# Fewer filler products at the start, and the left-over rows of the last four batches in output order

## The chip, the cores and the metric

The kernel runs on one core of one Trainium2 chip. Its engines work side by side, each on its own stream of instructions: TensorE (PE) for matrix products, VectorE (DVE) and ScalarE (ACT) for element-wise work, GpSimd (POOL) and SyncE (SP), which here mostly issue transfers. ACT also has a queue from which it issues transfers. The metric is the device time of one execution in microseconds (us). The kernel before takes 240.45 us, the median of 3 runs from 239.67 to 241.16.

## The reference

```python
B, H, S, D = q.shape                  # 8, 8, 576, 64
m = 32
scale = 1.0 / np.sqrt(D)
q_lm = q.reshape(B, H, m, S // m, D).mean(axis=3)
k_lm = k.reshape(B, H, m, S // m, D).mean(axis=3)
A  = softmax(scale * q    @ k_lm.T)
Bm = softmax(scale * q_lm @ k_lm.T)
C  = softmax(scale * q_lm @ k.T)
Z = Bm.T / (norm1(Bm) * norminf(Bm) + 1e-06)
for _ in range(6):
    Z = 2 * Z - Z @ Bm @ Z
attn = A @ Z @ C @ v
x = attn.transpose(0, 2, 1, 3).reshape(B * S, H * D)    # 4608 x 512
h = x @ w_in                                            # 512 x 2048
g = h * (1.0 / (1.0 + np.exp(-h)))
out = g @ w_out                                         # 2048 x 512, float32
```

This is an attention with 32 landmarks per head, whose small inverse is found by six iterations, followed by a two-layer network with a silu between the layers.

## The kernel before

Every step is an operation with a name (`A(name, engines, emit, deps, ...)`), and a text, `SEQUENCE`, lists the names in the order in which each engine gets its instructions; nothing reorders them afterwards. A word `*n` in it puts n filler products on PE: a product of a tile of zeros (`zer`, 128x128) with 256 columns of zeros into a PSUM bank that is not otherwise used at that time. A word such as `c21@5740.0/DVE` picks the engine where there is a choice.

Per batch (the number behind the dot), `attn` builds transposed queries and keys, landmark sums (`lms`, `lmc`, `ltr`, `lmT`), the small softmax (`sb`, `pb`), the exponentials of A (`A`, `Ax`) and of C (`C`, `Cx`), the normalisation of A (`S` on PE, `Ln` and `Rs` on ACT, `etn` on DVE), and the iterations (`ns` on PE, `nsd` and `fb` on DVE). From `cv`, `wc`, `zbd`, `zt` comes a small matrix per head, and `m0` to `m3` multiply it with the first layer's weights, so that the first layer is one product of `etn` with `m`. `layer1` runs that product, in operations `h0` to `h15` for 512 of the 576 rows of a batch; `g0` to `g15` are the silu of each on ACT, written to `gm`.

A batch has 576 = 32 x 18 rows: row 18 l + j belongs to landmark l and place j. The 512 rows are j from 0 to 15. The 64 left-over rows, j = 16 and 17, go through `hx0` and `hx8`, and the silu `gx0` and `gx8` writes them to `gx`, where four batches stand side by side: 64 columns each, first the 32 rows of j = 16, then those of j = 17. After batches 3 and 7 the second layer takes `gx` as a group of 256 rows.

The second layer (`layer2_pair`) takes 256 rows as an upper and a lower half of 128 and halves of the weights, and forms the output with seven products (`p1` to `p7`) instead of eight, with sums of operands on DVE (`ss0` to `ss3`). The copies and additions c1, u2, c11, c12, c5, c22, c21 bring the products from PSUM into two output tiles of 128 x 512: c11 completes the left 256 columns of the first tile, c12 its right columns, c22 the right columns of the second tile, c21 its left columns. Transfers (`store`) then write rows to memory. Each takes 32 rows with the same j, since consecutive l lie 18 output rows apart. For the last batch's tiles, four transfers per tile alternate between the queues of SP and ACT (`spread`), and for the very last pair, that of `gx` (named 5740 and 5741), the first tile goes as eight transfers of 32 rows x 256 columns and the second as four of 32 x 512.

Transfers of SP and ACT share eight completion counters: each transfer gets one, and is issued only when the earlier transfer with that counter has landed.

The fillers before stand at these places: 15 at the very start, 6 and 6 during the first transposes, 1 ahead of `ltr0.0`, 6 ahead of `sb.0`, 5 ahead of `C.0`, 2 ahead of `ltr1.1`, and from there to `h4.0` 22 in ten places among the iterations of batch 0 and the exponentials of batch 1, and 1 more ahead of `h13.0`; 64 in all.

Of the kernel before, what the change touches and what calls it, by code (L numbers as in the profile page):

```python
# [10 lines left out]
AF = mybir.ActivationFunctionType  # L11
# [13 lines left out]
lmT0.0/ACT *6 sb.0 pb.0 trc014.0/DVE trc09.0/DVE A.0 Ax01.0 Ax00.0 Ax10.0 Ax11.0 *5 C.0 Cx01.0  # L25
# [6 lines left out]
tr10.1 trc10.1/ACT tr15.1 *2 ltr1.1 lmT1.1/ACT fb20.0 nsd21.0 etn1.0 trc15.1/DVE ns20.0 fb31.0 *3  # L32
ns31.0 ctm10.0 trc114.1/ACT etn0.0 nsd31.0 sb.1 pb.1 *1 A.1 Ax01.1 Ax00.1 nsd20.0 fb30.0 pbs.1
wrc.0 *1 ns30.0 nsd30.0 ctc10.0/DVE fb40.0 pbr.1 fb41.0 bmx.1 bmt.1 wi3b1 Ax11.1 Ax10.1 *5 C.1
Cx00.1 Cx11.1 Cx01.1 *1 ns40.0 nsd40.0 ns41.0 nsd41.0 fb50.0 fb51.0 cv0.0 cv1.0 wc.0 S01.1 Ln01.1
ns50.0 nsd50.0 *2 ns51.0 bbd.1 nsd51.0 zbd.0 S11.1 Ln11.1 S00.1 Ln00.1 wi2b0 wi2b1 wi2a ldv0.1
ldv1.1 *5 zt.0 ztc.0/DVE S10.1 ctm00.1 ctc00.1/DVE Rs0.1 Ln10.1 Cx10.1 *2 m1.0 mc11.0/ACT
mc10.0/DVE m0.0 f0.1 mc01.0/DVE mc00.0/ACT *1 ctm10.1 ctc10.1/DVE Rs1.1 csb.1 *1 h4.0 n1.1 m3.0
nrm.1 stz.1 stf0.1 mc31.0/DVE fb00.1 g4.0 mc30.0/DVE h2.0 g2.0 h6.0 g6.0 h0.0 g0.0 h3.0 ns00.1
wrc.1 nsd00.1 fb10.1 h5.0 g5.0 m2.0 mc21.0/ACT mc20.0/DVE *1 h13.0 g13.0 ns10.1 nsd10.1 fb20.1  # L40
h15.0 hx0.0 g15.0 ns20.1 nsd20.1 fb30.1 h9.0 g9.0 h11.0 g11.0 etn0.1 ns30.1 nsd30.1 fb40.1 hx8.0
gx8.0 g3.0 h8.0 h12.0 g12.0 etn1.1 ns40.1 nsd40.1 fb50.1 gx0.0 h10.0 g10.0 ld1.2 tr15.2
trc15.2/DVE h14.0 g14.0 ns50.1 nsd50.1 zbd.1 ldv2.1 cv0.1 wc.1 tr114.2 trc114.2/DVE tr19.2
trc19.2/DVE zt.1 g8.0 ztc.1/ACT tr10.2 trc10.2/DVE lra1.2 h7.0 g7.0 m3.1 mc31.1/ACT mc30.1/ACT
m1.1 mc11.1/DVE mc10.1/ACT h1.0 g1.0 ld0.2 tr00.2 lrb1.2 tr09.2 tr014.2 trc014.2/DVE tr05.2
trc05.2/DVE trc09.2/DVE lrc1.2 trc00.2/ACT h12.1 g12.1 h7.1 g7.1 h15.1 m2.1 mc20.1/ACT m0.1
mc00.1/ACT mc21.1/ACT mc01.1/ACT wo0 o0@5001.0 h14.1 g14.1 g15.1 o0@5000.0 fold lrd1.2 lra0.2
lrb0.2 lrc0.2 lrd0.2 h11.1 g11.1 ltr0.2 ltr1.2 lmT1.2/DVE lmT0.2/ACT ss00@5020.0 ss10@5020.0
ss20@5020.0 ss30@5020.0 wo1 h5.1 o1@5000.0 sb.2 pb.2 pbs.2 pbr.2 bmx.2 bmt.2 wo2 wt00 bbd.2 h8.1
h3.1 o1@5001.0 o2@5000.0 wo3 o2@5001.0 wt01 g8.1 csb.2 o3@5001.0 oc@5001.0/ACT g3.1 g5.1 n1.2  # L50
nrm.2 stz.2 o3@5000.0 hx8.1 f0.2 gx8.1 h0.1 g0.1 oc@5000.0/ACT h2.1 h10.1 g10.1 h4.1 h1.1 g2.1
g1.1 wt11 wt21 stf0.2 fb00.2 ns00.2 h13.1 g13.1 wt31 nsd00.2 fb10.2 wt10 wt20 wt30 p1@5020.0
c1@5020.0/ACT ns10.2 nsd10.2 fb20.2 h9.1 h6.1 g4.1 g9.1 g6.1 ss00@5100.0 p5@5020.0 c5@5020.0/DVE
hx0.1 gx0.1 ss10@5100.0 l1done.0 C.2 Cx00.2 Cx10.2 p6@5020.0 u2@5020.0/DVE ld100.3 ld101.3 ld110.3
ld111.3 ldv1.3 xt10.3<ldv1.3 xt11.3<ldv1.3 ns20.2 nsd20.2 ss20@5100.0 p3@5020.0 c12@5020.0
p7@5020.0 ld000.3 ld001.3 ld010.3 ld011.3 xt01.3<ldv1.3 xt00.3<ldv1.3 ldv0.2 ldv2.2 ldv1.2
l1done.1 A.2 Ax01.2 Cx11.2 ct1.2<ldv1.3 Ax10.2 Ax11.2 p1@5100.0 c1@5100.0/ACT Ax00.2 Cx01.2
ct0.2<ldv1.3 os@5000.0 ld100.4<ct0.2 ld101.4 ld110.4 ld111.4 lra1.3 fb30.2 ns30.2 p2@5020.0
ss30@5100.0 lrb1.3 os@5001.0 S10.2 S11.2 Ln11.2 Ln10.2 Rs1.2 p6@5100.0 S01.2 Ln01.2 S00.2 Ln00.2
p5@5100.0 nsd30.2 lrc1.3 fb40.2 lrd1.3 ltr1.3 c22@5020.0 lra0.3 u2@5100.0/DVE lrb0.3 p4@5020.0  # L60
ns40.2 lrc0.3 lrd0.3 ltr0.3 c11@5020.0 etn1.2 nsd40.2 c5@5100.0/ACT p3@5100.0 Rs0.2 lmT1.3/ACT
etn0.2 lmT0.3/ACT sb.3 c12@5100.0 c21@5020.0/ACT p7@5100.0 pb.3 pbs.3 pbr.3 fb50.2 A.3 Ax11.3
cv0.2 ldv1.4<xt00.3 c22@5100.0 wrc.2 wc.2 ld000.4<xt00.3 ld001.4 ld010.4 ld011.4 ldv0.3 ldv2.3
ldv2.4<xt00.3 ns50.2 nsd50.2 Ax10.3 Ax00.3 S11.3 Ln11.3 Ax01.3 p2@5100.0 C.3 Cx00.3 Cx01.3 Cx10.3
zbd.2 zt.2 ztc.2/ACT S10.3 Ln10.3 p4@5100.0 Cx11.3 ss00@5120.0 c11@5100.0 os@5100.0 ss10@5120.0
ss20@5120.0 p1@5120.0 S01.3 Ln01.3 m3.2 mc31.2/ACT bmx.3 wrc.3 mc30.2/DVE c21@5100.0/ACT os@5101.0
ct1.3<ldv1.4 m2.2 mc21.2/DVE mc20.2/ACT bmt.3 p5@5120.0 S00.3 m0.2 m1.2 mc11.2/DVE csb.3 bbd.3
n1.3 nrm.3 stz.3 c1@5120.0/ACT p6@5120.0 u2@5120.0/DVE mc01.2/ACT mc10.2/ACT Rs1.3 Ln00.3 Rs0.3
mc00.2/ACT h14.2 f0.3 h12.2 p2@5120.0 stf0.3 fb00.3 ns00.3 nsd00.3 c5@5120.0/DVE fb10.3 c11@5120.0
g12.2 p7@5120.0 h7.2 g7.2 ns10.3 nsd10.3 h4.2 h5.2 h8.2 g8.2 g5.2 fb20.3 ns20.3 h10.2 g10.2  # L70
c22@5120.0 p4@5120.0 c21@5120.0/ACT nsd20.3 fb30.3 ns30.3 hx0.2 nsd30.3 fb40.3 h15.2 gx0.2 g15.2
ns40.3 nsd40.3 ct0.3<ldv1.4 xt00.4<ldv1.4 h9.2 g9.2 g14.2 h1.2 h0.2 g1.2 g0.2 fb50.3 ss30@5120.0
ns50.3 nsd50.3 zbd.3 h11.2 g11.2 h13.2 h3.2 cv0.3 h2.2 wc.3 g4.2 g13.2 g3.2 etn1.3 zt.3 ztc.3/DVE
etn0.3 p3@5120.0 c12@5120.0 m3.3 mc30.3/ACT m0.3 mc01.3/DVE mc00.3/ACT m2.3 mc21.3/ACT m1.3
mc20.3/ACT hx8.2 g2.2 h6.2 g6.2 mc31.3/DVE h12.3 gx8.2 h3.3 h10.3 mc10.3/DVE mc11.3/DVE h7.3 h2.3
g2.3 h4.3 g4.3 g10.3 h13.3 h5.3 g5.3 hx8.3 gx8.3 g13.3 h9.3 h11.3 g7.3 h14.3 h6.3 g6.3 g11.3
p1@5200.0 g3.3 h8.3 g8.3 ss00@5200.0 p5@5200.0 hx0.3 g14.3 g9.3 ss00@5220.0 xt11.4<ldv1.4
xt01.4<ldv1.4 xt10.4<ldv1.4 ld100.5<xt10.4 ld101.5 ld110.5 ld111.5 ldv0.4 ldv1.5 ld000.5 ld001.5
# [175 lines left out]
def kernel(  # L254
# [43 lines left out]
    def bank(o, i=0):  # L298
        return banks[o.slot[i]]
# [54 lines left out]
    A = P.add  # L354
# [546 lines left out]
    def layer1(b):  # L901
# [5 lines left out]
        for dc in range(NDC):  # L907
# [20 lines left out]
            if dc % 8 == 7:  # L928
                d0 = dc - 7
                cell = {}  # L930

                def xm(e, d0=d0, cell=cell):
                    ps = bank(cell["o"]).rearrange("p (c x) -> p c x", c=8)
                    for d in range(8):
                        for g in range(NG):
                            mm(ps[:, d].rearrange("p (c x) -> p c x", c=2),
                               m_sb[:, g, (d0 + d) * 128:(d0 + d + 1) * 128],
                               etc[:, g, :, 256:288], start=(g == 0), stop=(g == 1))
                o = cell["o"] = A(f"hx{d0}.{b}", [("PE", mm_us(64, 16))], xm,
                                  etn_ops[b] + m_ops[b, d0 // 4] + m_ops[b, dc // 4]  # L940
                                  + l2_last.get(("x", b // 4 - 1), []), p + 0.5, psum=1, cls="L1")
                pes.append(o)
                c = (b % 4) * 64
                gx_ops[b].append(A(
                    f"gx{d0}.{b}", [("ACT", act_us(512))],
                    lambda e, d0=d0, cell=cell, c=c: nc.scalar.activation(  # L946
                        out=gx[:, d0:d0 + 8, c:c + 64],
                        in_=bank(cell["o"]).rearrange("p (c x) -> p c x", c=8), func=AF.Silu),
                    [o], p + 0.5, table="silu").reads(o))
# [36 lines left out]
    def store(e, t, place, m, cols=slice(0, DMODEL)):  # L986
# [101 lines left out]
    def layer2_batch(b):  # L1088
# [10 lines left out]
        if b % 4 == 3:  # L1099
# [3 lines left out]
                [[(x, j) for x in (y, y + 1) for j in (J - 2, J - 1)] for y in (b - 3, b - 1)],  # L1103
# [69 lines left out]
```

## Time and profile before

| | |
|---|---|
| median of the runs | 240.45 us |
| the profiled execution's own time | 239.41 us |
| its span, first to last instruction | 237.4 us |
| PE busy | 231.4 us, 2948 products |
| DVE busy | 183.0 us |
| ACT busy | 182.1 us |
| the 64 fillers | 1.1 to 31.0 us |
| written to memory | 9.44 MB |

A span is divided in the profile's page into 40 slices with the busy share of each engine, and the chain of work that ended last is followed back from the last instruction. PE counts as busy while it waits with a product begun, so its share is to be read together with the waits of the engines that use its results. Times in the timeline are from the span's start. In a timeline row stand start, duration, engine, line, operation, output and inputs, shape and count, and behind it in brackets how long the engine had idled and for what. In a row of stretches stand, for each engine, its busy time and number of instructions, then the granted clock of PE, the busy share of the transfer engines and GB/s. `SPq` and `ACTq` are the queues of transfers of SP and ACT.

### The profile page before, as it was taken

The numbers are of one execution on the slowest core, as the hardware profiler recorded it, in microseconds if no ns is written. First come the engines' busy times: TensorE is split into PE (matmuls) and PEld (weight loads), VectorE is DVE, ScalarE is ACT, GpSimd is POOL, SyncE is SP. The second block draws the span as 40 slices with busy tenths as digits, with TensorE's granted clock in tenths as the row PEclk, the third lists the DMA queues.
The fourth block names the chain that finished last, engine by engine and source line by source line (L and its number), as shares of the span: only waits on it lengthen the run. The fifth ranks groups of instructions, "written<-read, shape, count | busy, mean of one in ns | idle before, by whom it ended". The sixth has DMA issues, their size and how long they took to land.

```text
span 237.4 us, 7504 instructions
## 1 busy us (share of the span) xinstructions
PE 231.4 (97%) x2948; PEld 164.5 (69%) x2948; DVE 183.0 (77%) x508; ACT 182.1 (77%) x433; POOL 49.6 (21%) x89
## 2 busy tenths in 40 slices
PE   7999999999999999999999999999999999999993
PEld 5987556456877645687878655768876746789882
DVE  2689989898998669949999789858998665447752
ACT  3599999989889988996857998999779897812200
POOL 0936641240055004403060084000000000000000
PEclk9999999999999999999999999999999999999998
DMA  6999999999989996999999999995427450012355
GB/s 251 267 203 186 204 210 207 207 206 179 166 149 205 222 230 128 189 191 174 200 154 214 178 157 231 202 171 121 91 68 100 115 122 0 4 44 48 76 136 144
DMA packets 56163, 37.72 MB, mean 159 GB/s; under 512 B 37056, under 2 KB 47552, under 8 KB 56128
## 3 DMA queue, kind: packets, MB, share of 16 engines
q0 software_dynamic: 15168, 17.18, 44.4%
q1 hardware_dynamic: 40288, 19.28, 39.3%
q10 hardware_dynamic: 672, 0.79, 1.1%
q8 instruction: 23, 0.38, 0.7%
q14 instruction: 12, 0.10, 0.1%
HBM read 36.70 MB, written 9.44 MB: 194 GB/s over the span
## 4 chain that ended last, share of the span: by engine, by line
PE 84%; DMA 6%; ACT 4%; DVE 2%; SPq 2%; issue 1%; DVEq 0%; ACTq 0%
PE ps L337 81%; DMA out_dram<-ost 5%; PE ps L527 3%; SPq L988 2%; DMA gm<-in_k_dram 1%; DVE etn L772 1%; ACT L1126 1%; ACT ln L767 1%; ACT m L347 0%; ACT pb L652 0%; ACT ln L763 0%; ACT qk L347 0%; ACT et L753 0%; PE ps L813 0%; ACT gx L946 0%
## 5 line engine op out<-in xcount | busy, mean ns | idle before, releaser
L923 ACT ACTIVATE gm<-ps 128x512 f16<-128x512 f32 x128 | 68.1, 626 | 4.6 <-PE ps L337 4.4
L337 PE MATMUL ps<-etn,m 128*128 128x64 bf16 (+1 forms) x512 | 71.2, 286 | 0.1
L337 PEld LDWEIGHTS <-gm 128*128 128x128 f16 x512 | 48.8, 98 | 11.0 <-issue 1.0
L337 PE MATMUL ps<-w_out_sb,gm 128*128 128x256 f16 (+1 forms) x392 | 52.5, 281 | 0.0
L337 PEld LDWEIGHTS <-m 128*128 128x128 bf16 x512 | 31.4, 98 | 23.1 <-issue 2.8
L337 PEld LDWEIGHTS <-ss 128*128 128x128 f16 x408 | 38.4, 98 | 7.8 <-issue 1.8
L337 PE MATMUL ps<-wt,ss 128*128 128x256 f16 x272 | 34.9, 273 | 0.0
L1046 DVE TENSOR_TENSOR ost<-ost,ps 128x256 f32<-128x256 f32 x51 | 20.7, 416 | 10.5 <-PE ps L337 7.2
L347 ACT COPY ost<-ps 128x256 f32<-128x256 f32 (+1 forms) x45 | 17.3, 391 | 12.0 <-PE ps L337 11.8
L349 DVE CAST m<-ps 128x512 bf16<-128x512 f32 x29 | 18.8, 685 | 3.6 <-PE ps L337 3.5
L347 ACT CAST m<-ps 128x512 bf16<-128x512 f32 x35 | 18.9, 607 | 2.1 <-PE ps L337 2.1
L418 POOL DMA_DIRECT2D v<-in_v_dram x24 | 14.7, 621 | 27.9 <-PE ps L337 17.1
L721 DVE SCALAR_TENSOR_TENSOR st<-st,ps 128x128 bf16<-128x128 bf16 (+2 forms) x54 | 13.7, 257 | 7.8 <-PE ps L337 6.8
L401 POOL DMA_DIRECT2D qk<-in_k_dram x20 | 10.6, 545 | 36.6 <-DMA qT<-qk 16.5
L337 PE MATMUL ps<-w_out_sb,ss 128*128 128x256 f16 x136 | 17.6, 273 | 0.0
L349 DVE COPY ost<-ps 128x256 f32<-128x256 f32 x25 | 10.5, 421 | 7.1 <-PE ps L337 6.6
L946 ACT ACTIVATE gx<-ps 128x512 f16<-128x512 f32 x16 | 9.9, 622 | 7.5 <-PE ps L337 7.3
L337 PE MATMUL ps<-wt,gm 128*128 128x256 f16 x120 | 15.5, 272 | 0.0
L696 DVE TENSOR_TENSOR fb<-st,hmask 128x256 bf16<-128x256 bf16 (+1 forms) x54 | 14.5, 274 | 1.1
L401 POOL DMA_DIRECT2D qk<-in_q_dram x20 | 10.6, 548 | 20.3 <-issue 12.2
L798 ACT ACTIVATE ce<-ps 128x288 bf16<-128x288 f32 x32 | 12.9, 420 | 2.3 <-PE ps L337 2.3
L763 ACT ACTIVATE ln<-ps 128x288 f32<-128x288 f32 x32 | 12.3, 428 | 3.0 <-PE ps L337 2.8
(93 smaller groups left out, 347.6 us busy)
## 6 DMA issues: line engine op xcount, KB each, us to landing
out_dram<-ost SPq DMA_DIRECT2D x130, 64.0 KB, 2.0
v<-in_v_dram POOLq DMA_DIRECT2D x24, 192.0 KB, 7.7
qk<-in_k_dram POOLq DMA_DIRECT2D x20, 144.0 KB, 6.3
qk<-in_q_dram POOLq DMA_DIRECT2D x20, 144.0 KB, 6.1
w_out_sb<-in_moe_w_out_dram POOLq DMA_DIRECT2D x4, 512.0 KB, 15.1
gm<-in_k_dram SPq DMA_DIRECT2D x2, 576.0 KB, 3.9
gm<-in_q_dram SPq DMA_DIRECT2D x2, 576.0 KB, 6.8
qk<-in_q_dram POOLq DMA_DIRECT2D x2, 576.0 KB, 8.5
```

What stands on the lines that cost most here:

```text
L337: nc.tensor.matmul(out=out_ap, lhsT=lhsT, rhs=rhs, start=start, stop=stop, skip_group_check=True)
L347: nc.scalar.copy(out=out, in_=in_)
L349: nc.vector.tensor_copy(out=out, in_=in_)
L401: lambda e, t=t, g=g, h=h, src=src: nc.gpsimd.dma_start(out=qk_r[b % 2][64 * h:64 * h + 64, t, g].rearrange("p j d -> p (j d)"), in_=src[b ...
L418: lambda e, a=a: nc.gpsimd.dma_start(out=v_r[b % 2][a * L:(a + 1) * L, :, :], in_=v[b].rearrange("h (l a x) d -> a l h (x d)", l=L, a=VA)[ ...
L696: nc.vector.tensor_tensor(out=fb[it % 2][:, g0:g1], in0=bc(sr[it % 3][:, g0:g1, 0:L], 4, 2), in1=bc(hmask, n, 1), op=OP.mult), [o], 14.5 + ...
L721: nc.vector.scalar_tensor_tensor(out=s2[:, g0:g1, lo:SW], in0=s[:, g0:g1, lo:SW], scalar=2.0, in1=ps[:, 0:NG * SW].rearrange("p (g x) -> p ...
L763: lambda e, g=g, c=c, ln=ln: nc.scalar.activation(out=ln[:, c], in_=bank(me["S", g, c])[:, 0:HS], func=AF.Ln),
L798: nc.scalar.activation(out=ce[:, :, 0:VP].rearrange("p (i c) (a l) -> p c a i l", c=2, a=VA)[:, c], in_=bank(me["C"], 2 * g + c)[:, 0:HS]. ...
L923: lambda e, dc=dc, cell=cell: nc.scalar.activation(out=gm[:, dc, :], in_=bank(cell["o"]), func=AF.Silu),
L946: lambda e, d0=d0, cell=cell, c=c: nc.scalar.activation(out=gx[:, d0:d0 + 8, c:c + 64], in_=bank(cell["o"]).rearrange("p (c x) -> p c x", ...
L1046: nc.vector.tensor_tensor(out=out_, in0=x, in1=y, op=OP.add)
```

## The change

Three edits. First, 23 of the 64 fillers leave the order, in twelve places between `sb.0` and `h4.0`: ahead of `sb.0` 6 become 3, of `C.0` 5 become 3, of `ns31.0` 3 become 1, of `A.1` 1 goes, of `ns30.0` 1 goes, of `C.1` 5 become 2, of `ns40.0` 1 goes, of `ns51.0` 2 go, of `zt.0` 5 become 1, of `m1.0` 2 go, of `ctm10.1` 1 goes, of `h4.0` 1 goes. (The words that name the change say 24.) Second, the silu of the left-over rows of batches 4 to 7 writes them with j fastest: column 2 l + (j - 16) of the batch's 64; for that it reads its PSUM bank in pairs that lie 32 floats apart. Rows 18 l + 16 and 18 l + 17 are then neighbours in the tile as in the output. Third, the last pair's tiles leave as transfers of 64 rows (one batch's) x 256 columns, two for each column half, each half as soon as its copy or addition is done.

```diff
-lmT0.0/ACT *6 sb.0 pb.0 trc014.0/DVE trc09.0/DVE A.0 Ax01.0 Ax00.0 Ax10.0 Ax11.0 *5 C.0 Cx01.0
+lmT0.0/ACT *3 sb.0 pb.0 trc014.0/DVE trc09.0/DVE A.0 Ax01.0 Ax00.0 Ax10.0 Ax11.0 *3 C.0 Cx01.0
...
-os3@5721.0/SP os2@5721.0/ACT os00@5740.0/SP os01@5740.0/ACT os02@5740.0/SP os03@5740.0/ACT
-p7@5740.0 c5@5740.0/DVE p3@5740.0 c22@5740.0 c12@5740.0 os10@5740.0/SP os11@5740.0/ACT
-os13@5740.0/SP os12@5740.0/ACT p4@5740.0 c21@5740.0/DVE os0@5741.0/SP os1@5741.0/ACT os2@5741.0/SP
-os3@5741.0/ACT l1done.4
+os3@5721.0/SP os2@5721.0/ACT os00@5740.0/SP os01@5740.0/ACT p7@5740.0 c5@5740.0/DVE p3@5740.0
+c22@5740.0 os10@5741.0/SP os11@5741.0/ACT c12@5740.0 os10@5740.0/SP os11@5740.0/ACT p4@5740.0
+c21@5740.0/DVE os00@5741.0/SP os01@5741.0/ACT l1done.4
...
-                        out=gx[:, d0:d0 + 8, c:c + 64],
-                        in_=bank(cell["o"]).rearrange("p (c x) -> p c x", c=8), func=AF.Silu),
+                        out=gx[:, d0:d0 + 8, c:c + 64].rearrange("p d (x c) -> p d x c", c=2)
+                        if b >= B - 4 else gx[:, d0:d0 + 8, c:c + 64],
+                        in_=bank(cell["o"]).rearrange("p (d c x) -> p d x c", d=8, c=2)
+                        if b >= B - 4 else bank(cell["o"]).rearrange("p (c x) -> p c x", c=8),
+                        func=AF.Silu),
...
+    def store_rows(e, t, place, m, cols=slice(0, DMODEL)):
+        return {"SP": nc.sync, "ACT": nc.scalar}[e].dma_start(
+            out=out[place[m] * S:(place[m] + 1) * S, cols].rearrange(
+                "(l j) n -> l j n", j=J)[:, J - 2:J],
+            in_=t[2 * L * m:2 * L * m + 2 * L, cols])
...
-            if spread == 2 and not h:
+            if spread == 2:
                 ost_st[i] = [A(f"os{u}{m}@{prio + h}", [("SP", 0.46), ("ACT", 0.46)],
-                               lambda e, m=m, t=t, u=u, h=h: store(e, t, places[h], m, slice(
+                               lambda e, m=m, t=t, u=u, h=h: store_rows(e, t, places[h], m, slice(
                                    HM * u, HM * u + HM)), [dep[u]], prio + 0.1 * u,
-                               dma=0.1, lag=1.5) for u in range(2) for m in range(4)]
+                               dma=0.16, lag=1.5) for u in range(2) for m in range(2)]
...
-                [[(x, j) for x in (y, y + 1) for j in (J - 2, J - 1)] for y in (b - 3, b - 1)],
+                [[y, y + 1] if b == B - 1 else [(x, j) for x in (y, y + 1) for j in (J - 2, J - 1)]
+                 for y in (b - 3, b - 1)],
```

More of the change, by code (lines that the diff above doesn't have):

```diff
@@ L37 @@
[L37 to L78, printed above, removed]
@@ new lines @@
+fb30.2 ns30.2 p2@5020.0 ss30@5100.0 lrb1.3 os@5001.0 S10.2 S11.2 Ln11.2 Ln10.2 Rs1.2 p6@5100.0
+S01.2 Ln01.2 S00.2 Ln00.2 p5@5100.0 nsd30.2 lrc1.3 fb40.2 lrd1.3 ltr1.3 c22@5020.0 lra0.3
+u2@5100.0/DVE lrb0.3 p4@5020.0 ns40.2 lrc0.3 lrd0.3 ltr0.3 c11@5020.0 etn1.2 nsd40.2 c5@5100.0/ACT
+p3@5100.0 Rs0.2 lmT1.3/ACT etn0.2 lmT0.3/ACT sb.3 c12@5100.0 c21@5020.0/ACT p7@5100.0 pb.3 pbs.3
+pbr.3 fb50.2 A.3 Ax11.3 cv0.2 ldv1.4<xt00.3 c22@5100.0 wrc.2 wc.2 ld000.4<xt00.3 ld001.4 ld010.4
+ld011.4 ldv0.3 ldv2.3 ldv2.4<xt00.3 ns50.2 nsd50.2 Ax10.3 Ax00.3 S11.3 Ln11.3 Ax01.3 p2@5100.0 C.3
```

53 lines of the change are left out of this document (44 added, 9 removed).

## The prediction

> **What bounds the kernel now.** I read the page first: shares, slices and the chain of work that ended last. TensorE (PE) is named busy for 97% of the span and holds 84% of the chain. That share says little: a PE that waits inside its stream is counted busy, so each of the two changed places is read from its own stretch.
>
> ```profile
> PE 231.4 (97%) x2948; PEld 164.5 (69%) x2948; DVE 183.0 (77%) x508; ACT 182.1 (77%) x433; POOL 49.6 (21%) x89
> PE 84%; DMA 6%; ACT 4%; DVE 2%; SPq 2%; issue 1%; DVEq 0%; ACTq 0%
> ```
>
> The first place is the head, 11.8 to 28 us, where the removed fillers stand. The timeline of PE gives a filler's price: five take 0.71 us and six 0.82, so one more costs 0.11 us. The words of the change say 24, the written order says 64 before and 41 after, so 23 go, 23 x 0.11 = 2.5 us of PE time.
>
> ```profile
> 1.06 3.38 PE L337 MATMUL ps<-zer 128*128 128x256 bf16 x15 [1.06 <-DVE zer L445]
> 11.79 0.82 PE L337 MATMUL ps<-zer 128*128 128x256 bf16 x6
> 21.80 0.71 PE L337 MATMUL ps<-zer 128*128 128x256 bf16 x5
> ```
>
> Is PE the limit there? The stretches say no: ScalarE (ACT) is busy 7.55 of 8.20 us and 7.63 of 8.00, and the list of ACT's waits from 11.5 to 31 us has three rows, 1.1 us in all, the first two of them before ACT runs full. ACT's chain then goes through a table load (28.23) and a silu (29.52), and only at 30.17 does PE take over.
>
> ```profile
> 11.80:20.00 8.20, 8.20 (x186) 6.80 (x184) 7.08 (x30) 7.55 (x25) 3.99 (x7) 1.00 1.19 191
> 20.00:28.00 8.00, 8.00 (x172) 5.07 (x171) 7.37 (x30) 7.63 (x24) 4.40 (x8) 1.00 1.24 204
> ...
> ACT pb L647 <- PE ps L337: 0.5, 1, 0.5
> ACT lmT L347 <- PE ps L337: 0.4, 1, 0.4
> ACT et L753 <- PE ps L337: 0.2, 1, 0.2
> ...
> 28.23 0.58 ACT L923
> ...
> 29.52 0.61 ACT gm L923
> ...
> 30.17 5.53 PE ps L337 x65
> ```
>
> The second place is the end. The last product runs from 232.35, its copy (c21) from 233.42 to 233.84, and then only transfers are left.
>
> ```profile
> 232.35 1.04 PE L337 MATMUL ps<-wt,gx 128*128 128x256 f16 x8
> ...
> 233.42 0.42 DVE L349 COPY ost<-ps 128x256 f32<-128x256 f32 x1 [0.45 <-PE ps L337]
> ...
> L988 SPq DMA_DIRECT2D out_dram<-ost x1: 427/427/427, 234.8 to 234.8; - x1
> DMA to landing us min/median/max: 1.7/1.7/1.7
> ...
> L988 ACTq DMA_DIRECT2D out_dram<-ost x2: 377/404/432, 233.9 to 234.3; - x2
> DMA to landing us min/median/max: 1.7/1.9/2.0
> ```
>
> ACT's queue issues its two transfers of the last tile at 233.9 and 234.3; SP's queue, held by earlier transfers, issues its last at 234.8, and that lands 1.7 us later, at 236.5. From there to the span's end is 0.9 us of closing.
>
> **The change part by part.**
>
> *The fillers: at most 0.37 us, taken as 0.2.* With PE not the limit, the 2.5 us are nearly all idle time made visible. What is on ACT's path is a filler that delays a product on which ACT waits. Two of ACT's waits are of that kind, and the same picture stands at both: the next products use a part of the array (64*32), and start 0.20 us after the start of the last full-width filler.
>
> ```profile
> 11.99 0.37 ACT L347 CAST lmT<-ps 128x256 bf16<-128x256 f32 x1 [0.42 <-PE ps L337]
> 12.53 0.29 PEld L337 LDWEIGHTS <-lmT 64*32 64x32 bf16 x24 [0.21 <-ACT lmT L347]
> ...
> 20.56 0.64 ACT L347 COPY qT<-ps 128x512 bf16<-128x512 bf16 x1
> ...
> 21.06 0.28 PE L337 MATMUL ps<-zer 128*128 128x256 bf16 x1
> 21.28 0.44 PE L337 MATMUL ps<-qT,lmT 64*32 64x288 bf16 x16
> ...
> 21.66 0.71 ACT L753 ACTIVATE et<-ps 128x288 bf16<-128x288 f32 x2 [0.25 <-PE ps L337]
> ```
>
> At sb.0 the sixth filler starts at 11.79 + 5 x 0.11 = 12.34 and the product at 12.53, though its operand is ready at 12.36; with three fillers it can start near 12.41, 0.12 earlier. At A.1 the one filler goes; half of A.1 needs nothing that ACT still writes and can start near 21.06, so ACT's wait of 0.25 may close; the other half needs the copy that ends at 20.56 + 0.64 = 21.20. Together at most 0.37. The other ten sites give nothing: behind them ACT is busy with exponentials and logarithms when PE delivers, and that cover would have to vanish before their 0.11 us each count. Half of 0.37, because VectorE (7.37 of 8.00 us) is next: the left-inverse iterations in it feed m.0 and through it ACT's copies. Ends: 0 to 0.37 gained by this step; below nothing only by the clock, a rival below.
>
> *The silu of the left-over rows (gx): taken as 0.* Eight of the sixteen gx activations, those of batches 4 to 7, now read PSUM in pairs 32 floats apart, and write in one run as before. No row reads PSUM like that. The nearest are plain: activations that write in scattered runs of 32 (L798) cost what the ones in one run cost (L753).
>
> ```profile
> L798 ACT ACTIVATE ce<-ps 128x288 bf16<-128x288 f32 x32 | 12.9, 420 | 2.3 <-PE ps L337 2.3
> L753 ACT ACTIVATE et<-ps 128x288 bf16<-128x288 f32 x32 | 11.3, 418 | 2.1 <-PE ps L337 1.5 <-DVE etn L772 0.6
> L946 ACT ACTIVATE gx<-ps 128x512 f16<-128x512 f32 x16 | 9.9, 622 | 7.5 <-PE ps L337 7.3
> ```
>
> So zero is the near end. The far end is two turns for each element, which adds the 0.51 us by which back-to-back silus of this size follow each other (eight in 4.07 us). A gain has no mechanism: the elements are as many. What the far end costs is worked out as a rival.
>
> ```profile
> 148.23 2.56 ACT L923 ACTIVATE gm<-ps 128x512 f16<-128x512 f32 x5 [0.24 <-PE ps L337]
> ...
> 150.64 0.64 ACT L946 ACTIVATE gx<-ps 128x512 f16<-128x512 f32 x1
> ...
> 152.07 0.68 ACT L946 ACTIVATE gx<-ps 128x512 f16<-128x512 f32 x1
> ...
> 185.88 0.65 ACT L946 ACTIVATE gx<-ps 128x512 f16<-128x512 f32 x1
> ...
> 192.01 4.07 ACT L923 ACTIVATE gm<-ps 128x512 f16<-128x512 f32 x8
> ...
> 207.16 0.60 ACT L946 ACTIVATE gx<-ps 128x512 f16<-128x512 f32 x1 [0.83 <-PE ps L337]
> ```
>
> *The last pair's transfers: 0.7 us earlier.* Twelve transfers (eight of 32 rows x 256 columns, four of 32 x 512) become eight of 64 rows x 256. An issue takes 0.31 to 0.45 us for the 32-row shapes of the rows below and above, with no order by size; I give the new shape 0.43. There are four issues less, two per queue. The right half of the upper tile now leaves after c22, during the last two products, and behind c21 remains one transfer per queue instead of two. Each transfer also waits for the earlier one that used its completion counter (eight counters go round over both queues): that is why SP was late. In the changed order the last two follow counters whose transfers left at 231.3 or before; transfers at the end take 1.7 to 2.0, so they are free by 233.4. Both queues are then waiting when c21 ends: SP's two transfers ahead of the last follow the counters that set the old starts at 232.8 and 233.4, and the second is issued by 233.4 + 0.43 = 233.83; ACT's queue, which ran ahead of SP's, is done sooner. Nothing but these transfers is queued behind them. So the last issues start near 233.87, 0.9 us before SP's 234.8.
>
> ```profile
> SPq L988 <- DMA out_dram<-ost: 1.8, 4, 0.9
> ...
> L988 SPq DMA_DIRECT2D out_dram<-ost x1: 315/315/315, 232.8 to 232.8; - x1
> ...
> L988 SPq DMA_DIRECT2D out_dram<-ost x2: 315/384/452, 233.4 to 233.8; - x2
> ...
> out_dram<-ost ACTq DMA_DIRECT2D x4, 32.0 KB, 1.9
> out_dram<-ost SPq DMA_DIRECT2D x4, 32.0 KB, 1.6
> ```
>
> Landing: a transfer of 64 KB in runs of 1 KB is not in the trace; 64 KB in 2 KB runs takes 1.7 on SP and up to 2.0 on ACT (the last two of each, above), 32 KB in 1 KB runs 1.6 and 1.9. The later queue decides: 233.87 + 2.0 = 235.87, against 236.5, a gain of 0.6; if ACT's transfer also gets 1.7, because half the bytes share the engines, 0.9. I take 0.7. Ends: landing 1.5 gives 1.1 gained; landing 2.6 gives nothing, 3.4 a loss of 0.8. The Trainium skill, "DMA: Bandwidth & Descriptors", section "Anatomy of one DMA — SWDGE (gpsimd) path", gives a fixed 2.0 us plus bytes at 436 GB/s, for the other kind of queue; by it 64 KB take an estimated 2.15 us and the gain here would be 0.45, but the rows with 1.7 to 2.0 decide.
>
> **Sum.** The profiled execution took 239.41 us (span 237.4). Less 0.2 and 0.7 that is 238.5. The median of the runs shown is 240.45, 1.04 above it; the same difference of 0.9 taken from it gives **239.6 us**, 0.4% less, and well under the 1% or so that a measurement of this kernel can tell from no change.
>
> **The rivals.**
>
> *The silu gets slower (ends slower than before).* If a gx takes 0.5 us more, the place that pays is around 146 to 156 us and at 185.9. The gx at 150.64 and 152.07 stand in an unbroken row on ACT ahead of a table load and the softmax of a later batch, on which PE waits, and the second is in the chain itself; with two more just before 148.23, where ACT idles 0.24 us, and the one at 185.9 the most is 4 x 0.5 + 0.5 - 0.24 = 2.3 us, the least the two of the chain, 1.0; I take 1.5, so 239.55 + 1.5 = 241.1. The three from 207.16 on cost nothing: ACT has room there (0.83 us of idle ahead of the first). It turns the whole change into a loss from 0.45 us per gx on. For it: no row shows such a read to be free. Against it: nothing but the scattered writes. The Trainium skill, "Advanced Engine Details and Errata", section "Memory Cachelines", says PSUM lines hold two floats and each two neighbours should lie together for best throughput; by that rule the pairs 32 floats apart take this rival's side, and no row of the trace tests it, so it keeps a large chance, 0.25.
>
> *The clock falls.* The fillers keep the array at work. The array starts slow: the first 15 fillers take 3.38/15 = 0.225 us each, later ones 0.11. At the end the granted clock is at half from 235.5 on, 2.1 us after the last product's end (232.35 + 1.04 = 233.39).
>
> ```profile
> 235.50:236.00 0.50, 0.00 (x0) 0.00 (x0) 0.00 (x0) 0.00 (x0) 0.00 (x0) 0.50 0.94 275
> ```
>
> The largest cut at one place is four fillers, a hole of 0.44 us, far under 2.1; but if some thin stretch counts as idle, products from 25 to 30 us run at half speed, some 3 us more of PE work of which ACT's table load of 1.28 covers a part: 2 to 3 us lost, 239.55 + 2.5 = 242.1. Chance 0.08. The Trainium skill, "TensorE: Matmul & The Clock Gate", section "HAM oscillation — how this bites in real kernels", asks for no idle gap over about 3.4 us; by that rule the clock stays, and the trace's 2.1 us is shorter than the figure.
>
> *PE is the limit in the head after all.* Then all 2.5 us are gained: 240.45 - 2.5 - 0.7 = 237.25. ACT's short list of waits speaks against it; 0.05.
>
> *The end does not move*, because 64 rows of 1 KB land at 2.6 us or because a counter still holds a queue: 240.45 - 0.2 = 240.25; 0.1.
>
> **How the numbers follow.** My forecast has 0.52; with the ends of its steps it runs from 239.0 to 240.4, and the repeats of before (239.67 to 241.16) spread by 0.7 about their median. Down to 238.4 and up to 241.5 takes in the unmoved end, the silu rival up to its 1.9 and half of that spread; left out are the full gain, most of the clock rival and the silu's far end, under 0.2. Faster by over 1% (under 238.05): the full gain and a little of the forecast, 0.08. Slower by over 1% (over 242.85): some of the clock rival and the silu's far end with an unmoved end, 0.08. The rest, 0.84, within 1%.
>
> **What would show it.** Head: PE idle appears between 12 and 27 us, ACT's waits shrink by 0.1 to 0.35 and the silu at 29.52 starts 0.2 earlier; a PEclk under 1.00 there or matmuls twice as long prove the clock rival. gx: the batches 4 to 7 at 0.62 us or near 1.1. End: last issue within 0.1 us of c21's end on both queues, landing in 2.0 or less, 2.9 us rather than 3.56 from c21 to the span's end. Wrong it would be made above all by a gx over 1 us, or by a stall in the middle that moves with the shifted start.

## The result, and the profile after

The changed kernel takes 241.99 us, the median of 6 runs (241.60 to 242.71), against 240.62 us for the kernel before (239.67 to 241.16). The ratio is 1.0061, with a 95% interval from 1.0036 to 1.0087. That is 1.4 us slower, where 239.6 was forecast, and outside the range of 238.4 to 241.5.

The page of the changed kernel, the rows that answer to those of the prediction, and one that it left out:

```profile
PE 231.2 (96%) x2925; PEld 163.6 (68%) x2925; DVE 182.8 (76%) x508; ACT 182.3 (76%) x433; POOL 49.5 (21%) x89
...
q8 instruction: 23, 0.38, 0.6%
...
PE 81%; DMA 10%; ACT 3%; POOL 2%; DVE 1%; issue 1%; SPq 0%; DVEq 0%
...
L944 ACT ACTIVATE gx<-ps 128x512 f16<-128x512 f32 x16 | 9.8, 622 | 7.5 <-PE ps L335 7.3
```

PE has 23 products less. The silu of the left-over rows costs 622 ns in the mean as before, though half of the 16 now read in pairs 32 floats apart (those eight take 0.59 to 0.68 us, the other eight 0.60 to 0.66). The row of q8 is a queue through which the core loads its instructions, 23 packets, and it will matter.

The profiled execution of the changed kernel took 242.35 us with a span of 240.2, before it was 239.41 and 237.4: 2.8 us more. The chain splits them into three. First the chain of the changed kernel (start, duration, what):

```profile
28.14 2.89 PE ps L335 x20
31.05 5.53 PE ps L335 x65
...
119.06 2.78 DMA ct<-ce
...
157.51 77.40 PE ps L335 x864
234.94 0.42 DVE ost L347
```

*The start: 0.88 us.* PE takes over at 31.05 instead of 30.17. This is not the doing of the removed fillers. The timeline of PE shows why, first before, then after (start, duration, and how many):

```profile
5.05 0.48 PE L337 MATMUL ps<-qk,idb 128*128 128x64 bf16 x6 [0.61 <-ACT qk L347]
...
6.86 0.82 PE L337 MATMUL ps<-zer 128*128 128x256 bf16 x6
```

```profile
5.30 0.48 PE L335 MATMUL ps<-qk,idb 128*128 128x64 bf16 x6 [0.86 <-ACT qk L345]
...
7.19 1.47 PE L335 MATMUL ps<-zer 128*128 128x256 bf16 x6
```

The first data arrive 0.25 us later, and the six fillers behind them, which both kernels have, take 0.82 us in one trace and 1.47 in the other: the array comes to full speed later (the granted clock is 1.00 in both all the while). All this lies ahead of the first removed filler. Both kinds of start occur with 64 fillers and with 41 (below), so it is taken as a draw of the single execution; what decides it stays open.

From 12 to 28 us the removed fillers do in part what the prediction said, idle time becomes visible (15.21 us busy in these two stretches, 16.20 before: 1.0 of the 2.5 us that it named):

```profile
11.80:20.00 8.20, 8.04 (x194) 6.63 (x191) 6.97 (x29) 6.87 (x24) 3.74 (x6) 1.00 1.20 194
20.00:28.00 8.00, 7.17 (x165) 4.50 (x162) 7.47 (x32) 7.95 (x26) 5.08 (x9) 1.00 1.24 204
```

*The middle: 0.64 us.* The lag of 0.88 at 31 us is 1.52 at 157.51 (155.99 before). On the way PE waits for a transposing transfer (`ct`, 119.06 in the chain), which the chain before does not have.

*The end: 1.28 us.* From c21's end (235.36) to the span's end there are 4.84 us, not the forecast 2.9, and not 3.56 as before. The transfers of the last 18 us (duration shortest/median/longest in ns, first and last start), first before, then after:

```profile
L988 SPq DMA_DIRECT2D out_dram<-ost x21: 314/420/516, 222.0 to 234.8; - x21
L988 ACTq DMA_DIRECT2D out_dram<-ost x14: 322/432/512, 226.0 to 234.3; - x14
```

```profile
L989 SPq DMA_DIRECT2D out_dram<-ost x16: 314/421/1440, 223.2 to 234.5; - x16
L989 ACTq DMA_DIRECT2D out_dram<-ost x8: 374/416/1429, 227.5 to 233.7; - x8
L994 ACTq DMA_DIRECT2D out_dram<-ost x4: 553/598/746, 234.4 to 236.7; - x4
L994 SPq DMA_DIRECT2D out_dram<-ost x4: 541/550/666, 235.0 to 237.0; - x4
...
DMA to landing us min/median/max: 1.6/1.9/4.0
```

Two things stand out. The new shape (L994) costs 0.54 to 0.75 us of queue time, not 0.43; the eight land in

```profile
DMA to landing us min/median/max: 2.0/2.1/2.3
```

And on each queue one issue of the old shape (L989) took over 1.4 us, 1.44 and 1.43. Both began at 231.74 and 231.77. The view of the transfers from 231.0 to 233.0, in 40 slices of 0.05 us (busy tenths of the 16 transfer engines), shows what else ran:

```profile
DMA  8629989899710000000000093899369989350000
...
q8 instruction: 1, 0.02, 4.9%
```

Just then a 16 KB block of instructions is loaded (4.9% of 16 engines' 2 us is 1.57 us of one engine), and for 0.55 us (the eleven zeros) nothing else moves. Narrow windows place the start of that load, the last of the 23, between 231.1 and 231.4 in the changed kernel, and between 226.6 and 227.0 before:

```profile
q8 instruction: 1, 0.02, 32.8%
```

```profile
q8 instruction: 1, 0.02, 23.7%
```

Each product is a load of weights and a multiplication, two instructions: 2948 x 2 / 23 = 256 of them per block, 64 bytes each, so the blocks are PE's. Counted in PE's own instructions the last three loads begin at the same places in all 14 traces, after 5288 to 5316, 5548 to 5566 and 5792 to 5804 of them. 23 products less put each later load 46 instructions, a fifth of a block, further on in the work. The Trainium skill, "Runtime: NRT & Kernel Launch", section "Instruction fetch mechanics", describes this: blocks of 16 KiB or 256 instructions, fetched through a queue of the engine's own, at a cost it calls mostly hidden. The trace agrees on the block; that it is hidden holds for PE, which in the kernel before has no gap of over 0.12 us after 33 us, and not for the transfers of others.

### The profile page after: what moved, and what is told of

Its sections match the earlier page's. It is cut to its first block, busy times and chain, and to the rows that moved or that the text cites. A ratio compares the mean times of both kernels' runs of the same rounds, so it can differ in the third digit from the quotient of the medians.

```text
span 240.2 us, 7456 instructions
## 1 busy us (share of the span) xinstructions
PE 231.2 (96%) x2925; PEld 163.6 (68%) x2925; DVE 182.8 (76%) x508; ACT 182.3 (76%) x433; POOL 49.5 (21%) x89
## 4 chain that ended last, share of the span: by engine, by line
PE 81%; DMA 10%; ACT 3%; POOL 2%; DVE 1%; issue 1%; SPq 0%; DVEq 0%
PE ps L335 80%; DMA w_in_sb<-in_moe_w_in_dram 7%; DMA gm<-in_k_dram 2%; ACT gm L921 1%; DMA ct<-ce 1%; PE ps L525 1%; POOL v L416 1%; POOL qk L409 1%; DVE etn L770 1%; ACT L1134 1%; POOL w_in_sb L427 1%; ACT gx L944 0%; ACT pb L650 0%; ACT et L751 0%; DVE ost L347 0%
```

## The experiments

In the table, *load* is how long ahead of c21's end the last block begins; *issue* the longest issue of a 32-row transfer that starts less than 7 us ahead of c21's end; *tail* the time from c21's end to the span's end; *waits* PE's gaps of over 0.12 us after 33 us, summed. These come from one profiled execution each, the ratios to the kernel before from the timed runs.

| kernel | products | load | issue | tail | waits | ratio (95%) |
|---|---|---|---|---|---|---|
| before | 2948 | 7.1 | 0.52 | 3.56 | 0 | 1 |
| before again | 2948 | 7.2 | 0.50 | 3.70 | 0 | |
| rows only | 2948 | 7.3 | 0.44 | 3.78 | 0 | 1.0006 (0.9976 to 1.0036) |
| fillers only + tiny | 2948 | 7.0 | 0.45 | 3.44 | 0 | 1.0017 (0.9999 to 1.0035) |
| after + tiny | 2948 | 6.8 | 0.44 | 3.78 | 0.15 | 0.9992 (0.9965 to 1.0020) |
| after + tiny, late | 2948 | 6.8 | 0.43 | 3.81 | 0.45 | 1.0026 (0.9989 to 1.0064) |
| after + half tiny | 2937 | 5.9 | 0.91 | 3.48 | 0.23 | 1.0014 (0.9989 to 1.0038) |
| fillers only | 2925 | 4.2 | 1.01 | 4.26 | 0.52 | 1.0035 (1.0008 to 1.0061) |
| before, wide fillers | 2925 | 4.1 | 0.74 | 4.23 | 1.60 | 1.0056 (1.0032 to 1.0080) |
| after | 2925 | 4.1 | 1.44 | 4.84 | 0.47 | 1.0061 (1.0036 to 1.0087) |
| after again | 2925 | 4.1 | 1.31 | 4.88 | 1.17 | |

**Each part alone, and both kernels again.** The first took only the 23 fillers out of the order (the first of its places is shown), with the old transfers; the second kept all 64 fillers and took the new row order and the new transfers.

```diff
-lmT0.0/ACT *6 sb.0 pb.0
+lmT0.0/ACT *3 sb.0 pb.0
...
```

> Before with only the 23 fillers taken out; rows and transfers as before. Theory A (the loss is in the last transfers, the head draws its time anew in every execution): 0 to 0.3 us faster than before, and 3.4 to 3.7 us from the end of c21 to the span's end. Theory B (fewer fillers slow the head): 0.6 to 1.5 us slower than before, with the first silu of batch 0 (29.5 before) at 30.2 or later in every execution.

> Before with only the new row order and the transfers of 64 rows; all 64 fillers stay. Theory A: 1.0 to 1.7 us slower than before, each of the eight last transfers 0.54 us or more in the issue, and over 4.3 us from the end of c21 to the span's end. Theory B: 0 to 0.9 us faster than before, as the prediction's step for the end had it.

> The kernel before, unchanged, for a second trace. If the head's time is a draw: the array's clock rises (fillers from 0.22 to 0.11 us each) at another moment than 6.3 us, and the first silu of batch 0 lies off 29.5 by 0.3 us or more. If it belongs to the order: 29.5 within 0.2.

> The changed kernel, unchanged, for a second trace. If the head is a draw: the first silu of batch 0 lies off the 30.4 of the first trace by 0.3 us or more. If the slow end belongs to the shape of the transfers: again 0.54 us or more for each issue and over 4.3 us from the end of c21 to the span's end; if a backlog of earlier transfers made it: under 4.0.

Measured: fillers only 241.29 us (1.0035), rows only 240.77 (1.0006), the two repeats, one execution each, 239.62 and 242.01. The part that was to cost nothing at worst carries more than half of the loss by these ratios, and the part blamed for the loss at first (the shape of the last transfers) alone makes no difference that can be measured. So theory A fails in both kernels. Theory B has the loss of the fillers, but the first silu, which it wanted late, comes early there (29.01), and for the rows its gain did not come. The repeats point both ways on the draw: before again the silu begins at 29.54, within 0.2 of 29.52, after again at 29.57, not at 30.40; that it is a draw rests on the other traces too, such as rows only with all 64 fillers and 30.43. In the fillers' trace the old transfers meet the load, from 229.5 to 232.4:

```profile
L984 ACTq DMA_DIRECT2D out_dram<-ost x4: 373/430/955, 230.2 to 232.1; - x4
L984 SPq DMA_DIRECT2D out_dram<-ost x2: 315/661/1007, 230.2 to 230.6; - x2
```

and its list of PE's waits from 60 to 157 us, empty before, has one row:

```profile
PE ps L333 <- DMA ct<-ce: 0.5, 1, 0.5
```

**Is it the filler time or the number of instructions?** Three kernels. In one the 23 removed fillers are replaced by tiny products (64 rows, 32 columns; the next one follows 0.025 to 0.04 us later): the number of before, nearly the time of after. In another, pairs of fillers become one of 512 columns: the time of before, the number of after. The third is the changed kernel with the tiny ones. A word `+n` in the order puts n of them, 23 in all; at these places they write to a bank that is not used. (The first edit is shown against the kernel with the filler edit alone.)

```diff
+    P.filler2 = Op("tiny", [("PE", 0.03)],
+                   lambda e: mm(banks[7][0:32, 0:32], zer[0:64, 0:32], zer[0:64, 0:32]))
-lmT0.0/ACT *3 sb.0 pb.0
+lmT0.0/ACT *3 +3 sb.0 pb.0
...
```

```diff
+    P.filler2 = Op("wide", [("PE", 0.22)],
+                   lambda e: mm(banks[7][:, 0:512].rearrange("p (a x) -> p a x", a=4), zer,
+                                bc(zer, 4, 1)))
-lmT0.0/ACT *6 sb.0 pb.0
+lmT0.0/ACT +3 sb.0 pb.0
...
```

> The kernel before with only the filler edit, but where a filler of 256 columns went a tiny product (64 rows, 32 columns of weights, 32 columns of data) stands in its place, so PE carries out as many instructions as in the kernel before and nearly as little filler time as after the edit. Theory L (instruction loads): PE's instructions come in blocks of 16 KB through a queue of their own (23 in a span), each load starts at a fixed place of the stream, and a load that meets the issue of a transfer holds that issue for about 1 us; 23 products less move every load later, the last from 226.8-227.5 us in the three traces with 64 fillers to 230.1-231.3 in the three with 41. Then here the last load is back near 226.5-227.5, no issue after 228 us takes over 0.6 us, c21's end to the span's end is 3.5-3.7 us, PE has no gap over 0.3 us between 33 and 157 us, and the time is 0.997 to 1.001 of the kernel before. Theory P (the filler time itself): PE gets ahead of the loads of data and waits for them later, and the shorter start changes the rest; then the gap of about 0.5 us near 120 us stays, and the time is 1.002 to 1.005 as in the run with the fillers alone (1.0035).

> The kernel before with 46 of its fillers, two at a time at the same place, each pair as one product of 512 columns: PE's filler time stays that of the kernel before at every place, and PE has 23 products less, as after the change. Theory L: the last instruction load falls near 230-231.5 us, two issues near 231 us take 0.9-1.4 us, c21's end to the span's end is 4.1-4.4 us instead of 3.56, the third transposing transfer of the second row of loads (near 83 us) is held for about 2.4 us instead of 1.3, and the time is 1.002 to 1.005 of the kernel before. Theory P: nothing changes, 0.999 to 1.001, and issues at the end take 0.31 to 0.45.

> The changed kernel with the 23 tiny products in the places of the removed fillers. Theory L: the last instruction load is back near 227 us, no issue of a whole-row transfer after 228 us is held over 0.6 us, c21's end to the span's end is 3.7-3.9 us instead of 4.84, PE has no gap over 0.3 us between 33 and 157 us, and the time is 0.998 to 1.002 of the kernel before, against 1.006 of the changed kernel. Theory P: the tail stays at 4.8 us and the time at 1.004 to 1.007.

The changed kernel with tiny products: 239.86 us, 0.9992. Its last load is back near 227.3, the issues from 229.5 to 232.4 are plain, and 1.1 us of tail are gone:

```profile
L993 SPq DMA_DIRECT2D out_dram<-ost x5: 314/369/436, 229.5 to 231.4; - x5
L993 ACTq DMA_DIRECT2D out_dram<-ost x4: 375/405/434, 230.1 to 231.4; - x4
```

The wide fillers: 241.27 us, 1.0056, just above the expected 1.002 to 1.005, slower with the old filler time at every place. In the same window:

```profile
L991 SPq DMA_DIRECT2D out_dram<-ost x4: 314/368/740, 230.0 to 232.1; - x4
L991 ACTq DMA_DIRECT2D out_dram<-ost x4: 375/404/717, 230.0 to 232.1; - x4
```

The held issues are 0.2 us shorter than expected, the tail (4.23) as expected. But its middle has a wait of another kind, 1.4 us for a landmark sum at 67 us, behind a transposing transfer issued at 60.53 that lands 5.9 us later:

```profile
PE ps L337 <- DVE rs L589: 1.4, 1, 1.4
```

No load meets that issue (the nearest begin at 52.4 and 63.4; the second falls into the time until the transfer lands), so this wait is not shown to come from the loads, and of this kernel's 1.4 us only the 0.6 at the end are. The fillers with tiny products took 240.40 us, 1.0017, between the two expectations (0.997 to 1.001, and 1.002 to 1.005): its time does not decide, its trace does, with a tail of 3.44, no held issue and no wait.

**Does the place of the load decide, or the work at the start?** The changed kernel with 12 tiny products, and with all 23 at one place late in the order:

```diff
-ss00@5600.0 p1@5600.0
+ss00@5600.0 +23 p1@5600.0
```

The late kernel serves for the time alone. By then bank 7 is in use too: in the order it holds half of `m2.7`, which `mc20.7` copies only after the tiny products have overwritten 32 x 32 of its numbers.

> The changed kernel with 12 tiny products instead of 23, at the first 12 of the places. Theory L (each instruction load starts at a fixed place of PE's stream and holds the issues that meet it): the last load moves half way, to 229-229.5 us, where it meets the pair of issues near 229.7 and holds these, and not those near 231.7; four transfers later the queues have caught up a part, so c21's end to the span's end is 3.8-4.6 us, between 3.78 with 23 tiny products and 4.84 with none, and the time 1.000 to 1.005 of the kernel before. If the number of products itself did it, whatever the place of the load, no issue would be held near 229.7.

> The changed kernel with the 23 tiny products all at one place late in PE's order, ahead of the first product of the second layer of batch 6 (near 190 us), instead of at the removed fillers' places. There PE is the limit, so they cost their own time, 23 x 0.035 = 0.8 us by the trace of the run with them at the start. Theory L: the loads of the first 190 us lie as in the changed kernel (the second transposing transfer near 84 us held for about 2.5 us, a PE wait of 0.4 to 1.2 us in the middle), the last loads as in the kernel before (last one 4 us ahead of where it met the issues, no whole-row issue over 0.6 us after it, c21's end to the span's end 3.5-3.9 us). Time: 1.0061 of the changed kernel, less 1.1 us at the end, plus 0.8: 1.003 to 1.006. If the number of products mattered only at the start, and not where the loads lie, the end stays at 4.84 us and the time is 1.007 to 1.011.

Half of them: 240.38 us, 1.0014. The load now begins at 229.0, and the pair of issues that is held is the earlier one, at 229.56 and 229.62, as expected (window 228.5 to 231):

```profile
L993 SPq DMA_DIRECT2D out_dram<-ost x3: 314/315/912, 229.2 to 230.9; - x3
L993 ACTq DMA_DIRECT2D out_dram<-ost x3: 374/374/854, 229.2 to 230.9; - x3
```

The tail came out at 3.48 us, below the expected 3.8 to 4.6: with two microseconds more, the queues make up the whole delay. Late: 240.90 us, 1.0026, just under the expected 1.003 to 1.006, with an interval too wide to decide on the time; the trace is plain. The tail is back at 3.81, no 32-row issue of the last 18 us is held,

```profile
L993 SPq DMA_DIRECT2D out_dram<-ost x16: 314/422/436, 223.7 to 233.2; - x16
L993 ACTq DMA_DIRECT2D out_dram<-ost x8: 375/414/434, 228.1 to 233.3; - x8
```

the 23 products add 0.79 us, as expected, where PE is the limit (the chain's last stretch of products is 78.19 us long, not 77.40), and the first 190 us look like those of the changed kernel: one transposing transfer held at 84.8, and PE's wait in the list from 60 to 157 us.

```profile
PE ps L337 <- DMA ct<-ce: 0.3, 1, 0.3
```

That transfer may be the middle's part of the story. Of four transposing transfers of queries and keys the second begins near 84 us; here are the rows that hold it, of before (first to third; the 3191 is the first, which waits for its data), after (first and second), after + tiny (second and third), and after + tiny late (first and second):

```profile
L551 SPq DMA_TRANSPOSE qT<-qk x3: 1291/1302/3191, 80.5 to 85.2; - x3
```

```profile
L549 SPq DMA_TRANSPOSE qT<-qk x2: 2522/2536/2549, 81.9 to 84.5; - x2
```

```profile
L553 SPq DMA_TRANSPOSE qT<-qk x2: 1291/1294/1298, 84.0 to 85.4; - x2
```

```profile
L553 SPq DMA_TRANSPOSE qT<-qk x2: 2444/2767/3090, 81.6 to 84.8; - x2
```

It took 2.41 to 2.55 us in all five traces whose start has 2925 products' worth of instructions, where a load begins at 82.8 to 85.1, and 1.29 to 1.30 in the nine others. These five have PE waits in the middle of 0.45 to 1.60 us, the others 0 to 0.23. That the one leads to the other (through SP's queue and the loads of later batches, which wait for the transposes) is read from the chain, not tested by itself, and the cause of the waits stays open: three of the five wait for `ct` near 121 us (0.26 to 0.52), after again for a copy by DVE (`lmT`) at 147 us (1.17), the wide fillers as told above; and near 102 us a transfer of this kind is held in the kernel before too, 2.33 us, with no wait behind it.

**Which issues does a load hold?** The 14 traces hold more of them than the end shows. Take the issues of output transfers that begin while a load runs, 0.2 us or more ahead of its end. All 85 that follow within 0.1 us on another issue of their queue are held: they take 0.66 to 1.89 us and end 0.14 to 0.51 us after the load. Of the 26 whose queue had been idle for 0.5 us or more, 25 are not held (0.31 to 0.38 us). So it is above: the first pair in a load is plain, the second held. The kernel before has such issues too, 1.82 us at 215.1 among them, and PE waits for none of them: the same delay costs only where a queue has no time left to make it up, as at the end.

**Can the end be made shorter?** With the rows in output order the last pair can leave in fewer pieces: six (the first tile as two of 64 rows x 512 columns), or four (the first tile as one of 128 x 512 after c12, the right half of the second as one of 128 x 256 after c22, its left half as two of 64 x 256 after c21). The last was run with all fillers and on the changed kernel with tiny products; its edit against the changed kernel:

```diff
+    def store_both(e, t, place, cols=slice(0, DMODEL)):
+        return {"SP": nc.sync, "ACT": nc.scalar}[e].dma_start(
+            out=out[place[0] * S:(place[1] + 1) * S, cols].rearrange(
+                "(b l j) n -> b l j n", b=2, j=J)[:, :, J - 2:J],
+            in_=t[:, cols])
-c22@5740.0 os10@5741.0/SP os11@5741.0/ACT c12@5740.0 os10@5740.0/SP os11@5740.0/ACT p4@5740.0
+c22@5740.0 os1@5741.0/ACT c12@5740.0 os@5740.0/SP p4@5740.0
```

> The kernel before with all 64 fillers, the new row order, and the last pair's tiles as six transfers: the first tile as two of 64 rows x 512 columns after its last addition, the second as four of 64 x 256 as in the change. The new shape's issue costs 0.54 to 0.75 us, so the eight transfers of the change keep SP's queue until 0.6 us after c21's end; with six, three per queue, both queues should be free when c21 ends. If the number of issues holds the end, c21's end to the span's end is 3.1-3.4 us (3.8 with the rows alone, 3.56 before) and the time 0.997 to 0.9995 of the kernel before. If the landing of the 64-row shape or the completion counters hold it, 3.7 or more, and 1.000 to 1.002.

> The kernel before with all 64 fillers, the new row order, and the last pair as four transfers: the first tile as one of 128 rows x 512 columns on SP after c12, the right half of the second as one of 128 x 256 on ACT after c22, its left half as two of 64 x 256, one per queue, after c21. The closing walks through the eight completion counters one after the other, 0.06 us each; the last transfer's counter stands at the end of that walk in the kernel before, four steps ahead of it with the change's eight transfers (0.24 us more after the last landing), and six ahead with six. With four it is at the end again. Expected if counters and issues hold the end: last bytes about 2.0 us after c21's end and 1.3 us from there to the span's end, 3.3 us in all (3.56 to 3.70 before, 3.78 with eight), time 0.997 to 1.000 of the kernel before. If the moved bytes hold it, last bytes at 2.3 or later and the time 0.999 to 1.002.

> The changed kernel with the 23 tiny products and the last pair as four transfers as in the run beside it: the sum of what the runs so far point to. The head gains 0.2 to 0.5 us as in the traces with 41 fillers that start early, the end 0.3, the instruction loads stay where they were: 0.995 to 0.999 of the kernel before. If the four large transfers hold the end, no better than with eight: 0.998 to 1.001.

Six: 240.23 us, 1.0013 (0.9986 to 1.0039), a tail of 3.79: no gain, although the last issues began 0.03 and 0.17 us after c21's end. (Its last load, 7.2 us ahead of that end, met an issue on ACT that took 2.22 us; the queue had made that up by then.) Four: tails of 3.30 and 3.29 as expected, but 240.43 us, 1.0015 (0.9990 to 1.0039), and 240.20 us, 1.0006 (0.9986 to 1.0026): the 0.3 to 0.5 us do not show in the times, both missed the gain that was expected of them, and no version is shown to beat the kernel before.

The rows-only trace says why the eight new transfers gain nothing. Half-microsecond stretches from c21's end on, before and then rows only (the last two numbers are the transfer engines' busy share and GB/s):

```profile
233.80:234.30 0.50, 0.00 (x0) 0.00 (x0) 0.05 (x1) 0.00 (x0) 0.00 (x0) 1.00 0.43 99
234.30:234.80 0.50, 0.00 (x0) 0.00 (x0) 0.00 (x0) 0.00 (x0) 0.00 (x0) 1.00 0.51 133
234.80:235.30 0.50, 0.00 (x0) 0.00 (x0) 0.00 (x0) 0.00 (x0) 0.00 (x0) 1.00 0.73 203
235.30:235.80 0.50, 0.00 (x0) 0.00 (x0) 0.00 (x0) 0.00 (x0) 0.00 (x0) 0.66 0.96 271
```

```profile
234.80:235.30 0.50, 0.00 (x0) 0.00 (x0) 0.00 (x0) 0.00 (x0) 0.00 (x0) 1.00 0.70 158
235.30:235.80 0.50, 0.00 (x0) 0.00 (x0) 0.00 (x0) 0.00 (x0) 0.00 (x0) 1.00 0.88 203
235.80:236.30 0.50, 0.00 (x0) 0.00 (x0) 0.00 (x0) 0.00 (x0) 0.00 (x0) 1.00 0.87 182
236.30:236.80 0.50, 0.00 (x0) 0.00 (x0) 0.00 (x0) 0.00 (x0) 0.00 (x0) 1.00 0.93 209
```

All of the new transfers move in runs of 1 KB, and with 0.93 busy the engines carry 209 GB/s, where the old ones' 2 KB runs reach 271 with 0.96. The last bytes arrive 2.28 us after c21's end (before 2.29). Then SP waits for the eight counters one after the other. The one that comes last is at the end of that walk before, and four transfers earlier in the round in rows only. The walk from 236.0 to 236.6 in the kernel before and from 237.15 to 237.75 in rows only; of the first row one wait ends after the last landing (236.49), of the second five (237.41):

```profile
L1168 SPq EVENT_SEMAPHORE  x3: 28/28/28, 236.2 to 236.5; - x3
```

```profile
L1174 SPq EVENT_SEMAPHORE  x6: 28/28/28, 237.2 to 237.7; - x6
```

From the last bytes to the span's end it is 1.27 us before, 1.50 with eight new transfers, 1.74 with six and 1.34 and 1.32 with four, where the round closes again.

## Why the prediction was wrong

**The fillers (0.2 gained, ends 0 to 0.37).** The gain itself is not at odds with the traces. In the traces where the array comes up early, the silu begins at 29.52 and 29.54 with 64 fillers and at 29.01 and 29.57 with 41. In those where it comes up late, 30.41, 30.43 and 30.96 stand against 30.09 and 30.40. The means differ by 0.24 and 0.35 us, with a scatter of up to 0.6 within a group. What failed is the sentence "below nothing only by the clock". It took a removed product for nothing but its time. A product is also 128 bytes in a stream that is loaded in blocks, and where the blocks are loaded moved for the whole rest of the kernel. Priced by the pairs of traces: with the old transfers the tail is 4.26 instead of 3.44 to 3.70, with the new ones 4.84 and 4.88 instead of 3.78 and 3.81, and in the middle PE waits 0.5 to 1.2 us. The prediction's last sentence named "a stall in the middle that moves with the shifted start"; such stalls came, but they go with the number of products ahead of them, not with the start: the changed kernel has them after an early start and a late one, and with tiny products 0.15 us.

**The silu (taken as 0).** Right: 622 ns before and after, and no changed one over 0.68 us. The rival that made the change slower this way is ruled out, and with it its price. The rule of the Trainium skill, "Advanced Engine Details and Errata", section "Memory Cachelines", that neighbours should lie together, does not show in these rows.

**The last transfers (0.7 gained).** Three terms failed. The issue was put at 0.43 us from rows of 32-row shapes and measured 0.54 to 0.76: with four per queue the last starts at 235.40, 0.6 us after c21's end, in the rows alone, and at 237.0 in the changed kernel, where the queues had also lost a microsecond to the load. The landing was put at 1.7 to 2.0 us and took 2.0 to 2.3. (The estimate of 2.15 us from the Trainium skill, "DMA: Bandwidth & Descriptors", section "Anatomy of one DMA — SWDGE (gpsimd) path", was nearer.) And the closing was put at 0.9 us from the last landing whatever the counters; their order costs 0.24 more. Together the part is worth nothing (1.0006) instead of 0.7. Of the 2.4 us by which the forecast was too low, that is 0.7; the loads are the rest, 1.7 us by the ratios of the changed kernel without and with tiny products (1.0061 - 0.9992, of 240). Each of the two figures is uncertain by some 0.7 to 0.9 us by its intervals, so that they add up to the whole is partly luck.

**The rivals.** *The clock falls*: not as put; the granted clock is 1.00 in the thin stretches. What varied was the array's rise before 9 us, in both kernels. *PE is the limit in the head*: no, the first silu moves by some 0.3 us and not by 2.5. *The end does not move*: nearest the truth for the transfers, but not for its reasons: they land in 2.0 to 2.3 us, not 2.6, and the queues are kept by the longer issues, which stand one behind the other (0.54 to 0.76 us), in the changed kernel after the load, and not by a counter. The rival that won, code loads that move, was not among them, though the row of q8 stood on the page.

**The range.** It reached up to 241.5 for the silu. The loss came from elsewhere and ended 0.5 us above it; the chance of 0.84 for within 1% still holds the result (0.6%).

## What to carry to other kernels

Adding or removing an engine's instructions moves every later block of its stream (shown here for PE); in a kernel that is limited by issue queues or by its last transfers, look where the blocks of 256 fall (the instruction queue in the transfers' view) before and after, and compare variants at an equal number of instructions. A change that should be neutral but is not can be tested in one run: give the count back with products too small to cost time. At the end of a kernel, price a new transfer's issue and the engines' rate at its run length from a run, and count what follows the last landing.

## What the runs showed of the hardware

- An issue by SP or ACT that follows directly on another while a 16 KB instruction block of PE is loaded is held until shortly after the load's end: in the last stretch 0.72 to 1.44 us instead of 0.31 to 0.45, on both queues at once (in one trace 2.22 us on ACT's alone, from 0.23 us ahead of the load on); for the second transposing transfer near 84 us 2.41 to 2.55 instead of 1.29. One whose queue was idle is not held (25 of 26). PE has no gap of over 0.12 us at any load after 33 us of the kernel before.
- A transfer of 64 rows x 1 KB costs a hardware queue 0.54 to 0.76 us to issue, one of 128 rows x 2 KB 0.68, one of 32 rows mostly 0.31 to 0.45 (single ones up to 0.63): by neither rows nor bytes alone.
- The array's rise to full speed, with the same 15 fillers from 1.06 us on, is done when the next fillers begin at 6.1 to 6.9 us in some executions, and not yet at 8 us in others; the later rise goes with about 1 us more at 30 us.
- PSUM read by ACT in pairs 32 floats apart costs the same as in one run, 0.59 to 0.68 us and 0.60 to 0.66 for 128 x 512.
